# Side work of the gate and up products placed at most one split to a product, its units further apart, and w2's begun seven products into the second half

## The chip, the cores and the metric

The kernel runs on one core of one Trainium2 chip. The metric is device time in microseconds. Everything is float32; the matmuls read float32r.

## The reference

```python
x = A_x                                   # 2048 x 1024
xn = layernorm(x)
# A: linear attention, 32 heads of 32, learned feature map
q, k, v = split(xn @ wqkv)
phi(t) = concat(softmax(t @ w_phi), softmax(-(t @ w_phi)))
s = (phi(q) (phi(k)^T v) / (phi(q) sum(phi(k)) + 1e-6)) @ wo
# B: gated feed-forward, 1024 -> 3584 -> 1024
h = silu(xn @ w1) * (xn @ w3)
g = silu(h @ w2)
out = x + s * g
```

## The kernel before

**Splits.** Every float32 operand of a large matmul is used as a high and a low part: ScalarE casts the source to float32r (line 91, `hi`), VectorE subtracts that from the source (line 92, `lo`), and TensorE makes three passes over the pairs (`PASSES`). The three large products (gate and up, keys and values, the product with w2) are done in seven block products instead of eight, as Strassen and Winograd do it, so sums of blocks are needed as operands as well.

**Stages.** (1) Normalise and transpose the first half of the tokens. (2) Gate and up: `for tb in range(2)` over the two halves of the tokens, and in each `for f in range(NF)` over 28 pieces of the weights. This is where the change lies. A pass of the inner loop is called a unit here, and counted from 0 in each half. (3) Keys and values (`heads`). (4) The product with w2. (5) Queries, attention and output.

**A unit** runs the seven products of `ORDER`, named here by their activation blocks: A11, A12, S2, S1, S3, S4, A22. Each has 12 matmuls of 128x128 on 128x512. A11, S2, S3 and A22 add up in one PSUM bank (`bankb`), and it is read between them: after A11 by ScalarE (line 588), after S2 by ScalarE (line 594), after S3 by VectorE (line 603), after A22 by ScalarE (line 610). S1 and S4 share `bankc`, which ScalarE reads after S1 (line 601) and VectorE after S4 (line 605). So S3 can't start before line 594 is done, S4 not before line 601, A22 not before line 603; between a product and the one that waits for its reading lies one other product.

In each product's code come, in this order: the 12 matmuls; one split of the next unit's weights (`next(b_gen)`, tile `bo`); the side work of this product (`after`); the reading of the bank. With `in_order` every engine runs its instructions in the order of the code, so a side split that waits on ScalarE or VectorE holds back the reading of the bank behind it. Side work that TensorE does stands ahead of the matmuls (`before`).

**Side work** is what later stages need, done between these products: `side_x` (normalise, transpose and split the second half's tokens into `xo_d`), `side_fold` (fold the feature map into the query and key weights), `side_kv` (sums and splits of the key and value weights into `wkv_d`), `side_w2` (the same for w2 into `w2_d`), `side_split` (splits of `wo` and some folded weights). It is put down by a table of steps: step 7 * unit + product, from 0 to 391, the second half from `HALF` = 196. `room(step, cost)` moves a split to the next step at which `base + took + cost` is at most 2.4; `base` is 0.7 for A12, S1 and S3, 1.4 for S2 and S4, 2.1 for A22, and 2.1 or 1.4 for A11 (even and odd units). The store of a split is issued by SyncE two steps later (line 406). GpSimd does the block sums (lines 126, 127, 230 to 236, 270, 272, 457, 459, 503, 505).

**Buffers.** Every split, of the weights or of side work, writes a tile of the pool `q`, which has 11 buffers of 4 KB in each partition. A `bo` tile is held until its product in the next unit; a side tile until its store has landed. Sources of side work lie in the pool `xp` (14 buffers, first half) and in 16 places of two `room` tiles (second half). SyncE issues every DMA, in order.

Of the kernel before, what the change touches and what calls it, by code (L numbers as in the profile page):

```python
# [28 lines left out]
def tile_kernel(ctx: ExitStack, tc: tile.TileContext, x, wkT, wqT, wv, wphi, wo, w1, w3, w2, out):  # L29
# [59 lines left out]
    def split(hi, lo, src, by=None):  # L89

        nc.scalar.copy(hi, src)  # L91
        (by or nc.vector).tensor_sub(lo, src, hi.bitcast(F))  # L92
# [78 lines left out]
    def blk(name):  # L171
        return xp.tile([P, 4, P], F, name=name, tag="x")

    def flat(t):
        return t.rearrange("p k t -> p (k t)")
# [7 lines left out]
    def load_x(t, halves):  # L183
        for h in range(2):
            nc.sync.dma_start(halves[h], x[t * P:(t + 1) * P, h * 512:(h + 1) * 512])
        return halves

    def stats(mv, j, xt):
        st = small.tile([P, 2, 6], F, name="st")
        for a in range(2):  # L190
            nc.vector.bn_stats(st[:, a, :], xt[a])
        nc.vector.bn_aggr(mv[:, j], st.rearrange("p a b -> p (a b)"))

    def rstd(mv):

        sd = small.tile([P, 4, 2], F, name="sd")
        var = mv[:, :, 1]
        nc.scalar.activation(sd[:, 0], var, AF.Sqrt, bias=eps_t)
        nc.vector.reciprocal(sd[:, 1], sd[:, 0])

        nc.vector.tensor_mul(sd[:, 2], sd[:, 1], sd[:, 1])
        nc.vector.scalar_tensor_tensor(sd[:, 3], var, EPS, sd[:, 2], op0=OP.add, op1=OP.mult)
        nc.vector.tensor_scalar(sd[:, 3], sd[:, 3], -0.5, 1.5, op0=OP.mult, op1=OP.add)
        nc.vector.tensor_mul(sd[:, 1], sd[:, 1], sd[:, 3])
        return sd

    def norm(mv, sd, j, xt):

        for a in range(2):
            nc.vector.tensor_scalar(xt[a], xt[a], mv[:, j, 0:1], sd[:, 1, j:j + 1], op0=OP.subtract, op1=OP.mult)  # L210

    def turn(half):
        pt = ps.tile([P, 4, P], F, name="pt", tag="tr", bufs=3)
        for k in range(4):
            nc.tensor.transpose(pt[:, k, :], half[:, k * P:(k + 1) * P], ident)
        return pt

    def raw_x(pt):
        xf = blk("xf")
        nc.scalar.copy(xf, pt)  # L220
        return xf

    def store_x(t, hf, xf):
        nc.sync.dma_start(xn_d[:, 4 * hf:4 * hf + 4, t * P:(t + 1) * P], xf)
# [78 lines left out]
    at_fold = 0  # L303
# [59 lines left out]
    def load_kv(c, k):  # L363
        r = [flat(blk("wkv")) for _ in range(4)]
        for n in range(2):
            nc.sync.dma_start(r[n], wk_d[c][k + 4 * n])
            nc.sync.dma_start(r[2 + n], wv[(k + 4 * n) * P:(k + 4 * n + 1) * P, c * 512:(c + 1) * 512])
        return r
# [14 lines left out]
    def at(step, f, d=after):  # L383
        d.setdefault(step, []).append(f)
# [4 lines left out]
    def room(step, cost):  # L389

        while True:
            f, j = divmod(step, 7)
            base = (2.1 if f % 2 == 0 else 1.4, 0.7, 1.4, 0.7, 0.7, 1.4, 2.1)[j]
            if base + took.get(step, 0) + cost <= 2.4:
                took[step] = took.get(step, 0) + cost
                return step
            step += 1

    def store_quad(step, d, src, name):

        step = room(step, 0.7)

        def f():
            t = qp.tile(list(src().shape[:1]) + [2] + list(src().shape[1:]), R, name=name, tag="q")
            split(t[:, 0], t[:, 1], src())
            at(step + 2, lambda: nc.sync.dma_start(d, t.bitcast(F)))
        at(step, f)
        return step

    def side_x(i, s0):  # L410
        xt, a, mv, sd, pts = [], {}, [], [], {}
        t0, t1 = pairs[i]

        def load():
            xt.extend(load_x(t, [flat(blk("xt")) for _ in range(2)]) for t in (t0, t1))
            mv.append(small.tile([P, 2, 2], F, name="mv", bufs=4))

        at(s0, load)
        at_ = s0 + 2
        for j in range(2):  # L420
            at_ = room(at_ + 1, 1.6)
            at(at_, lambda j=j: stats(mv[0], j, xt[j]))
        at_ = room(at_ + 1, 1.0)
        at(at_, lambda: sd.append(rstd(mv[0])))
        for j in range(2):
            at_ = room(at_ + 1, 1.0)
            at(at_, lambda j=j: norm(mv[0], sd[0], j, xt[j]))
        s1 = at_ + 1
        for m, (n, j, hf) in enumerate((("A11", 0, 0), ("A12", 0, 1), ("A21", 1, 0), ("A22", 1, 1))):
            at(s1 + m, lambda n=n, j=j, hf=hf: pts.update({n: turn(xt[j][hf])}), before)  # L430
            at(s1 + m, lambda n=n: a.update({n: raw_x(pts[n])}))
            at(s1 + m + 2, lambda n=n, j=j, hf=hf: store_x(pairs[i][j], hf, a[n]))
        at_ = s1
        for n in ("A11", "A12"):
            at_ = store_quad(at_ + 1, xo_d[1][n][:, i - 4], lambda n=n: a[n], f"xo{n}")
        at_ = max(at_ + 1, s1 + 7)
        for m in range(3):
            at(at_ + m, lambda m=m: a_sums(a, nc.gpsimd, m))
        at_ += 1
        for n in ("S3", "S1", "S2", "S4", "A22"):  # L440
            at_ = store_quad(at_ + 1, xo_d[1][n][:, i - 4], lambda n=n: a[n], f"xo{n}")

    def side_kv(c, k, s0):
        r, t2 = [], []
        at(s0, lambda: r.extend(load_kv(c, k)))

        def sums():
            t2.append(flat(blk("t2")))
            b_sums(r[0], r[2], r[3], t2[0])

        at(s0 + 4, sums)
        at_ = s0 + 5
        for n in BNAMES:
            src = {"B11": 0, "B21": 1, "T2": 4, "T1": 0, "T3": 2, "B22": 3, "T4": 1}[n]
            at_ = store_quad(at_ + 1, wkv_d[c][n][:, :, k], lambda src=src: (r + t2)[src], "wkvo")
            if n == "B11":
                at(at_, lambda: nc.gpsimd.tensor_sub(r[0], r[3], t2[0]))
            elif n == "B21":
                at(at_, lambda: nc.gpsimd.tensor_sub(r[1], r[1], t2[0]))

    def side_fold(m, s0):
        wT, k, c, d = folds[m]
        w = []
        at(s0, lambda: w.append(load_w(wT, k, c)))
        at(s0 + 4, lambda: w.append(flat(fold(w[0], c))), before)
        if m < 16:
            at(s0 + 4, lambda: nc.scalar.copy(flat(w[0]), w[1]))
            at(s0 + 6, lambda: nc.sync.dma_start(d, flat(w[0])))
        else:
            store_quad(s0 + 4, wqo_d[c][k], lambda: w[1], "wqo")  # L470

    def side_split(d, src, s0):
        r = []

        def load():
            r.append(blk2())
            nc.sync.dma_start(r[0], src)

        at(s0, load)
        store_quad(s0 + 4, d, lambda: r[0], "wso")  # L480

    def side_w2(kb, kk, s0):
        r = []

        def load():
            r.extend(blk2() for _ in range(4))
            for h in range(2):
                f = 4 * kb + 2 * kk + h
                for n in range(2):
                    nc.sync.dma_start(r[h + 2 * n], w2[f * P:(f + 1) * P, n * 512:(n + 1) * 512])  # L490

        def sums():
            r.append(blk2())
            b_sums(r[0], r[2], r[3], r[4])

        at(s0, load)
        at(s0 + 3, sums)
        at_ = s0 + 4
        for n in BNAMES:
            src = {"B11": 0, "B21": 1, "T2": 4, "T1": 0, "T3": 2, "B22": 3, "T4": 1}[n]  # L500
            at_ = store_quad(at_ + 1, w2_d[kb][n][:, kk], lambda src=src: r[src], "w2o")
            if n == "B11":
                at(at_, lambda: nc.gpsimd.tensor_sub(r[0], r[3], r[4]))
            elif n == "B21":
                at(at_, lambda: nc.gpsimd.tensor_sub(r[1], r[1], r[4]))
# [6 lines left out]
    hs = []  # L512
    FIRST_STEP = 7
    for i in range(4, 8):
        side_x(i, FIRST_STEP + 13 * (i - 4))
    for m in range(at_fold, len(folds)):
        side_fold(m, FIRST_STEP + 6 * (m - at_fold))
    for m in range(8):
        side_kv(m // 4, m % 4, FIRST_STEP + 48 + 13 * m)
    for m in range(28):  # L520
        side_store(m, FIRST_STEP + 2 + 5 * m)

    HALF = 7 * NF
    for u in range(2 * NKB):
        side_w2(u // 2, u % 2, HALF + 1 + 11 * u)

    late_splits = [(wqo_d[c][k], d) for _, k, c, d in folds[16:at_fold]]
    late_splits += [(wo_d[c][k], wo[k * P:(k + 1) * P, c * 512:(c + 1) * 512]) for c in range(2) for k in range(ND)]
    for m, (d, src) in enumerate(late_splits):
        side_split(d, src, HALF + 11 + 11 * (m // 2) + 5 * (m % 2))  # L530

    def store_h(d, b, t):
        nc.sync.dma_start(d[:, :, b].rearrange("i p t -> p i t"), t.rearrange("p (i t) -> p i t", i=4))
# [11 lines left out]
    for tb in range(2):  # L545
        early = {}
        for f in range(NF):
            last, step = f == NF - 1, HALF * tb + 7 * f
# [352 lines left out]
    for r, new in enumerate(steps):  # L901
        kb, i = new or (NKB, 0)
# [155 lines left out]
```

## Time and profile before

| | us |
|---|---|
| median of 3 runs | 2489.83 |
| lowest and highest | 2488.6, 2492.28 |
| span of the profiled execution, first to last instruction | 2486.2 |
| gate and up, first half from unit 1's A22 on (starts at 103.23) | 529.16 |
| gate and up, second half (starts at 632.39) | 558.74 |
| keys and values begin at | 1191.13 |

The profile gives no time of that execution beyond its span. Times in the trace are microseconds from the span's start. PE is TensorE's matmul, DVE VectorE, ACT ScalarE, POOL GpSimd, SP SyncE. In a row of the timeline stand the start, the duration, the engine, the line, the operation, what is written and read, how many were merged, and in brackets the idle time before it and what ended it.

### The profile page before, as it was taken

To read this page: it belongs to the slowest core of one execution; us is meant where nothing else is said; L and a number is where in the kernel's file an instruction comes from. 1 tells how busy PE (TensorE), PEld (TensorE's weight loads), DVE (VectorE), ACT (ScalarE), POOL (GpSimd) and SP (SyncE) were. 2 spreads that over 40 slices of the span, in tenths; PEclk is the share of its full clock that TensorE was granted. 3 is DMA by queue.
4 is the path that set the end of the run, shared out by engine and by line. 5 is a ranking of instruction groups with operands and counts; after the bars stand their busy time and mean duration, and the time that the engine had idled before them with its cause. 6 is when DMAs were issued, how large, how long until landed. Compare 5 with 4: busy or idle time off the path is not lost.

```text
span 2486.2 us, 35893 instructions
## 1 busy us (share of the span) xinstructions
PE 2410.0 (97%) x13648; PEld 1969.5 (79%) x13648; DVE 1715.1 (69%) x2573; ACT 894.9 (36%) x1555; POOL 672.1 (27%) x481
## 2 busy tenths in 40 slices
PE   5999899999899999999999999999999999999999
PEld 5788678888787787788788788788888887787877
DVE  8577767664577777764466566578787876777775
ACT  6455444443344455443111113422222243222221
POOL 1244445433354554432000000011111112222222
PEclk9999999999999999999999999999999999999999
DMA  8687897755987788744966864524444276322222
GB/s 293 219 273 262 283 296 250 248 185 175 292 286 265 279 285 297 256 162 164 361 245 259 298 210 146 193 106 167 169 178 167 98 287 236 98 71 91 77 83 71
DMA packets 300812, 521.02 MB, mean 210 GB/s; under 512 B 24544, under 2 KB 172000, under 8 KB 298848
## 3 DMA queue, kind: packets, MB, share of 16 engines
q1 hardware_dynamic: 300640, 518.74, 60.2%
q8 instruction: 107, 1.75, 0.3%
q14 instruction: 65, 0.53, 0.1%
HBM read 331.22 MB, written 187.44 MB: 209 GB/s over the span
## 4 chain that ended last, share of the span: by engine, by line
PE 82%; DMA 8%; DVE 4%; issue 2%; ACT 2%; SPq 1%; POOL 1%; ACTq 0%; DVEq 0%; POOLq 0%
PE bankb L575 18%; PE pm L100 14%; PE bankb L882 12%; PE bankc L575 8%; PE bankb L659 7%; PE bankc L882 6%; PE banka L575 4%; PE bankc L659 3%; PE banka L882 3%; PE banka L659 2%; DVE bo L92 1%; DMA wkv_d0T<-wkvo 1%; PE po L986 1%; PE pkv L644 1%; PE pt L980 1%
## 5 line engine op out<-in xcount | busy, mean ns | idle before, releaser
L92 DVE TENSOR_TENSOR bo<-rw,bo 128x512 fp32r<-128x512 f32 x336 | 294.0, 876 | 142.9 <-ACT bo L91 141.7
L91 ACT CAST bo<-rw 128x512 fp32r<-128x512 f32 x336 | 205.1, 621 | 74.7 <-PE bankb L575 16.8
L882 PE MATMUL bankb<-bo,as 128*128 128x512 f32 x816 | 201.6, 390 | 3.0 <-DVE acc L894 3.0
L270 POOL TENSOR_TENSOR rw<-rw,t 128x512 f32<-128x512 f32 x56 | 78.7, 1405 | 429.8 <-DVE bo L92 429.7
L892 POOL TENSOR_TENSOR acc<-acc,u 128x512 f32<-128x512 f32 x48 | 64.0, 1334 | 479.5 <-ACT u L891 381.7
L100 PE MATMUL pm<-wq,xh 128*128 128x512 f32 x768 | 185.2, 394 | 0.0
L882 PEld LDWEIGHTS bankb<-bo,as 128*128 128x128 f32 x816 | 153.3, 188 | 35.2 <-DVE acc L894 3.4
L575 PE MATMUL bankb<-op0A,bo 128*128 128x512 f32 x672 | 161.1, 393 | 12.1 <-DVE u L603 5.7
L575 PE MATMUL bankb<-op1S,bo 128*128 128x512 f32 x672 | 164.1, 393 | 5.9 <-ACT u L594 4.8
L575 PE MATMUL bankb<-op1A,bo 128*128 128x512 f32 x672 | 159.4, 393 | 10.4 <-DVE u L603 7.6
L575 PE MATMUL bankb<-op0S,bo 128*128 128x512 f32 x672 | 163.1, 391 | 6.3 <-ACT u L594 4.8
L100 PEld LDWEIGHTS pm<-wq,xh 128*128 128x128 f32 x768 | 142.0, 188 | 31.2 <-issue 2.8
L575 PE MATMUL bankc<-op0S,bo 128*128 128x512 f32 x672 | 162.8, 391 | 2.4 <-ACT u L601 2.4
L575 PE MATMUL bankc<-op1S,bo 128*128 128x512 f32 x672 | 161.9, 390 | 1.4 <-ACT u L601 1.4
L575 PEld LDWEIGHTS bankb<-op1A,bo 128*128 128x128 f32 x672 | 126.6, 189 | 39.4 <-DVE u L603 9.8
L575 PEld LDWEIGHTS bankb<-op0A,bo 128*128 128x128 f32 x672 | 125.0, 188 | 40.4 <-DVE u L603 7.9
L575 PEld LDWEIGHTS bankb<-op1S,bo 128*128 128x128 f32 x672 | 126.4, 189 | 35.4 <-ACT u L594 7.9
L575 PEld LDWEIGHTS bankb<-op0S,bo 128*128 128x128 f32 x672 | 125.2, 188 | 33.8 <-ACT u L594 6.3
L575 PEld LDWEIGHTS bankc<-op1S,bo 128*128 128x128 f32 x672 | 126.3, 188 | 28.6 <-ACT u L601 2.3
L575 PEld LDWEIGHTS bankc<-op0S,bo 128*128 128x128 f32 x672 | 125.6, 188 | 29.0 <-ACT u L601 3.2
L882 PE MATMUL bankc<-bo,as 128*128 128x512 f32 x576 | 147.3, 391 | 0.4 <-DVE as L92 0.4
L100 PE MATMUL pm<-wos,oT 128*128 128x512 f32 x576 | 136.3, 390 | 0.0
(201 smaller groups left out, 4681.9 us busy)
## 6 DMA issues: line engine op xcount, KB each, us to landing
rw<-in_w SPq DMA_DIRECT2D x112, 512.0 KB, 5.3
h_d<-h SPq DMA_DIRECT2D x112, 256.0 KB, 7.0
hr<-h_d SPq DMA_DIRECT2D x56, 512.0 KB, 3.5
xoS<-xo_d0S SPq DMA_DIRECT2D x32, 512.0 KB, 9.5
xoS<-xo_d1S SPq DMA_DIRECT2D x32, 512.0 KB, 3.3
room<-in_w SPq DMA_DIRECT2D x56, 256.0 KB, 6.3
xoA<-xo_d0A SPq DMA_DIRECT2D x24, 512.0 KB, 9.1
xoA<-xo_d1A SPq DMA_DIRECT2D x24, 512.0 KB, 3.8
```

The source lines that it names most:

```text
L91: nc.scalar.copy(hi, src)
L92: (by or nc.vector).tensor_sub(lo, src, hi.bitcast(F))
L100: nc.tensor.matmul(p, xT[dch][:, a], w(dch, b), start=n == 0, stop=n == 3 * ND - 1)
L270: nc.gpsimd.tensor_sub(b11, b22, t2)
L575: nc.tensor.matmul(bank[b], bo[bn][:, w, k], ao[an][:, u, k], start=first and n == 0, stop=LAST[b] == an and n == 11, skip_group_check=True)
L644: nc.tensor.matmul(pkv[sl, m], e[:, m // 4, (m % 4) * P + 32 * h:(m % 4) * P + 32 * h + 32], v[:, 4 * (m % 4) + h], start=first and m == 0 ...
L659: nc.tensor.matmul(bank[b], xo[an][:, u, k], wb[bn][:, w, k], start=an in ("A11", "A12", "S1") and n == 0, stop=LAST[b] == an and n == 11, ...
L882: nc.tensor.matmul(bank[b], t[:, u, pos + k], bos[kb, bn, k][:, w], start=first and n == 0, stop=LAST[b] == an and n == 5, skip_group_chec ...
L892: nc.gpsimd.tensor_add(c, c, u)
L980: nc.tensor.transpose(pt[:, g, :], e[:, (4 * q + g) * P:(4 * q + g + 1) * P], ident)
L986: nc.tensor.matmul(po[32 * g:32 * g + 32, hh, q * P:(q + 1) * P], kvu[sl, G * c + 4 * q + g], et[sl, g], start=True, stop=True, skip_group ...
```

## The change

The side work's limits and places are other numbers; no other line differs.

```diff
     def store_quad(step, d, src, name):
-        step = room(step, 0.7)
+        step = room(step, 1.0)
...
     for i in range(4, 8):
-        side_x(i, FIRST_STEP + 13 * (i - 4))
+        side_x(i, FIRST_STEP + 16 * (i - 4))
     for m in range(at_fold, len(folds)):
-        side_fold(m, FIRST_STEP + 6 * (m - at_fold))
+        side_fold(m, FIRST_STEP + 14 * (m - at_fold))
     for m in range(8):
-        side_kv(m // 4, m % 4, FIRST_STEP + 48 + 13 * m)
+        side_kv(m // 4, m % 4, FIRST_STEP + 60 + 12 * m)
...
     for u in range(2 * NKB):
-        side_w2(u // 2, u % 2, HALF + 1 + 11 * u)
+        side_w2(u // 2, u % 2, HALF + 7 + 12 * u)
...
-        side_split(d, src, HALF + 11 + 11 * (m // 2) + 5 * (m % 2))
+        side_split(d, src, HALF + 9 + 12 * (m // 2) + 6 * (m % 2))
```

With a cost of 0.7 a step with base 0.7 took two splits, one with base 1.4 one; with 1.0 both take one. Counted over the program's order, 22 products held two side splits before, 8 in the first half and 14 in the second; now none does. The first half has 94 side splits and the second 120 in both; the last one of the first half moves from unit 22 to unit 23, those of the second half lie in units 2 to 25 instead of 1 to 22.

The first place is ScalarE in unit 6 of the second half, from the reading of A11's bank (line 588) on; `w2o` and `wso` are side splits, `bo` the next unit's weights. Before:

```order
L588 COPY h0_6383<-bankb_6365 128x512
L91 CAST bo_6398<-rw_6205 128x512
L91 CAST w2o_6402<-room_5456 128x512
L91 CAST wso_6405<-room_5456 128x512
L591 ACTIVATE h0_6383<-h0_6383 128x512
L91 CAST bo_6422<-t2_6333 128x512
L91 CAST w2o_6425<-room_5455 128x512
L594 COPY u0_6429<-bankb_6365 128x512
L91 CAST bo_6447<-rw_6205 128x512
L91 CAST w2o_6450<-room_5455 128x512
L601 COPY u1_6459<-bankc_6434 128x512
```

The same place in the changed kernel:

```order
L588 COPY h0_6355<-bankb_6337 128x512
L91 CAST bo_6370<-rw_6175 128x512
L91 CAST w2o_6374<-room_5569 128x512
L591 ACTIVATE h0_6355<-h0_6355 128x512
L91 CAST bo_6395<-t2_6305 128x512
L91 CAST w2o_6398<-room_5570 128x512
L594 COPY u0_6401<-bankb_6337 128x512
L91 CAST bo_6419<-rw_6175 128x512
L91 CAST wso_6422<-room_5569 128x512
L601 COPY u1_6427<-bankc_6406 128x512
```

A12's part, between line 588 and line 591, has one side split where it had two.

The second place is SyncE's queue where the second half begins; `op1A22` is the last activation block of that half, `room` w2's sources, `h_d` the stores that free the tiles of lines 588 and 610. Before:

```order
L162 DMA op1A22_5372<-xo_d1A22_101 128x8x128 x4
L256 DMA rw_5416<-in_w1 128x1024
L257 DMA rw_5416<-in_w3 128x1024
L490 DMA room_5455<-in_w2 128x512 x4
L533 DMA h_d0_6_64<-h0_5279 128x4x128
L533 DMA h_d0_6_64<-h1_5256 128x4x128
L533 DMA h_d0_6_64<-h1_5412 128x4x128
L256 DMA rw_5557<-in_w1 128x1024
```

and now:

```order
L162 DMA op1A22_5372<-xo_d1A22_101 128x8x128 x4
L256 DMA rw_5416<-in_w1 128x1024
L257 DMA rw_5416<-in_w3 128x1024
L533 DMA h_d0_6_64<-h0_5279 128x4x128
L533 DMA h_d0_6_64<-h1_5256 128x4x128
L533 DMA h_d0_6_64<-h1_5412 128x4x128
L256 DMA rw_5549<-in_w1 128x1024
L257 DMA rw_5549<-in_w3 128x1024
L490 DMA room_5569<-in_w2 128x512 x4
```

w2's loads stand a unit later, behind the three stores and the next weights.

The third place is SyncE's queue at the third of the key and value loads (`wkv`, in the changed kernel at step 91, unit 13 of the first half), with what each DMA waits for. Before:

```order
L366 DMA wkv_2942<-wk_d0_2_118 128x512 [waits DMAHW5_49]
L367 DMA wkv_2944<-in_wv 128x512 [waits DMAHW6_49]
L366 DMA wkv_2943<-wk_d0_6_122 128x512 [waits DMAHW7_49]
L367 DMA wkv_2945<-in_wv 128x512 [waits DMAHW0_49]
L406 DMA wkv_d0B21_103<-wkvo_2893 256x1x512 [waits DMAHW1_49,DVE_49]
L406 DMA wkv_d0T2_104<-wkvo_2918 256x1x512 [waits DMAHW2_49,DVE_49]
```

and now:

```order
L240 DMA wr_3046<-in_wqT 128x512 [waits DMAHW4_49]
L366 DMA wkv_3048<-wk_d0_2_118 128x512 [waits DMAHW5_49]
L367 DMA wkv_3050<-in_wv 128x512 [waits DMAHW6_49]
L366 DMA wkv_3049<-wk_d0_6_122 128x512 [waits DMAHW7_49]
L367 DMA wkv_3051<-in_wv 128x512 [waits DMAHW4_49,DMAHW0_49,PE_49]
L406 DMA xo_d1A22_101<-xoA22_2997 128x1024 [waits DMAHW1_49]
L406 DMA wqo_d1_3_159<-wqo_3043 128x1024 [waits DMAHW2_49,DVE_49]
L533 DMA h_d0_3_61<-h0_2890 128x4x128 [waits DMAHW3_49]
```

The load of `wkv_3051` has got the buffer of `wr_3046`, which the fold of step 95 reads, so it waits for TensorE; before, none of the four loads did.

## The prediction

> **What bounds the kernel now.** I began with the page, then went to the stretches of gate and up, the only code that the change touches.
>
> ```profile
> span 2486.2 us, 35893 instructions
> PE 2410.0 (97%) x13648; PEld 1969.5 (79%) x13648; DVE 1715.1 (69%) x2573; ACT 894.9 (36%) x1555; POOL 672.1 (27%) x481
> ```
>
> TensorE is the bound, and no matmul is taken away. What can be won is only the time in which it doesn't run. The chain of waits shows how long a unit is when nothing holds it:
>
> ```profile
> 458.47 5.44 PE bankb L575 x24
> ...
> 610.79 5.44 PE bankb L575 x24
> ```
>
> Such a row is A22 with the next A11; the two are the first and the last of nine at equal distances, so a unit is (610.79 - 458.47) / 8 = 19.04 us and a product 2.72 us. Next, the windows of the first half from unit 1's A22 on, of a stretch of it, of the second half, and of the second half's thick part (columns: length, then busy time of PE, PEld, DVE, ACT, POOL, clock, DMA share, GB/s):
>
> ```profile
> 103.23:632.39 529.16, 516.56 (x2334) 425.72 (x2333) 356.07 (x471) 240.34 (x431) 222.64 (x152) 1.00 0.76 248
> 458.47:629.83 171.36, 171.36 (x757) 141.89 (x757) 95.60 (x129) 68.50 (x124) 62.66 (x44) 1.00 0.63 202
> 632.39:1191.13 558.74, 541.03 (x2353) 442.31 (x2352) 377.08 (x463) 249.80 (x449) 242.17 (x164) 0.99 0.73 255
> 700.00:1090.00 390.00, 379.24 (x1651) 309.49 (x1650) 292.30 (x356) 193.21 (x347) 193.53 (x128) 1.00 0.78 274
> ```
>
> Second half: 28 units x 19.04 = 533.1, so **25.6 us** are lost in 558.74. First half: 183 products x 2.72 = 497.8, so 31.4 are over, part of it TensorE's own side work:
>
> ```profile
> 118.22 0.60 PE L215 MATMUL pt<-ident,xt 128*128 128x128 f32 x4
> 118.58 3.00 PE L575 MATMUL bankb<-op0S,bo 128*128 128x512 f32 x12
> ...
> 150.55 1.05 PE L247 MATMUL pw<-bd,wr 128*128 128x128 f32 x8
> 151.36 1.85 PE L575 MATMUL banka<-op0A,bo 128*128 128x512 f32 x7
> ```
>
> A group of four transposes takes 0.36 and a fold 0.81, about 0.1 more each with the restart; 16 groups and 9 folds make some 16. That leaves **15.4 us** of waits in the first half. Together 41.0 us, 1.6% of the span, is all that placing side work can win here.
>
> **Who is waited for.** TensorE's timeline in the second half: its waits over 0.5 us but one, and (677.17) unit 1's A22:
>
> ```profile
> 651.65 5.70 PE L575 MATMUL bankb<-op1A,bo 128*128 128x512 f32 x24 [2.78 <-DMA op1A<-xo_d1A]
> 669.98 4.50 PE L575 MATMUL bankb<-op1S,bo 128*128 128x512 f32 x12 [3.39 <-ACT u L594]
> 677.17 5.60 PE L575 MATMUL bankb<-op1A,bo 128*128 128x512 f32 x24
> 710.70 3.03 PE L575 MATMUL bankb<-op1S,bo 128*128 128x512 f32 x12 [0.73 <-ACT u L594]
> 777.24 7.18 PE L575 MATMUL bankb<-op1A,bo 128*128 128x512 f32 x24 [2.36 <-DVE u L603]
> 831.33 3.04 PE L575 MATMUL bankb<-op1S,bo 128*128 128x512 f32 x12 [0.67 <-ACT u L594]
> 835.36 3.03 PE L575 MATMUL bankc<-op1S,bo 128*128 128x512 f32 x12 [0.99 <-ACT u L601]
> 877.89 5.74 PE L575 MATMUL bankb<-op1A,bo 128*128 128x512 f32 x24 [0.98 <-DVE u L603]
> 936.18 5.74 PE L575 MATMUL bankb<-op1A,bo 128*128 128x512 f32 x24 [0.83 <-DVE u L603]
> 996.61 5.74 PE L575 MATMUL bankb<-op1A,bo 128*128 128x512 f32 x24 [2.53 <-DVE u L603]
> 1016.82 5.78 PE L575 MATMUL bankb<-op1A,bo 128*128 128x512 f32 x24 [0.88 <-DVE u L603]
> ```
>
> All but the first of these waits are for a bank's reading. The rows down to 677.17 lie in units 0 and 1. The others lie in units 3, 6, 9 (twice), 11, 14, 17 and 18. Against the program's order: nine units hold two side splits in A12, namely 2, 3, 6, 9, 11, 13, 14, 17 and 18. Every stalled unit after unit 1 is one of these, and seven of the nine stall; four units with their double elsewhere (4, 7, 12, 15) and all eight units from 2 to 22 without one lose next to nothing. Unit 6 shows how:
>
> ```profile
> 774.74 0.62 ACT L91 CAST w2o<-room 128x512 fp32r<-128x512 f32 x1 [1.91 <-DMA w_d1T<-w2o]
> ```
>
> S3's side split waits for a `q` buffer, that is for an earlier store to land; S3's bank is read behind it, and A22 waits. The buffers say why one split more matters: a `bo` tile lives eight products (written in one, read a unit later), so eight of the 11 are taken and three are left. Stores take
>
> ```profile
> xo_d1S<-xoS SPq DMA_DIRECT2D x16, 512.0 KB, 3.7
> xo_d1A<-xoA SPq DMA_DIRECT2D x12, 512.0 KB, 7.1
> w_d1T<-w2o SPq DMA_DIRECT2D x8, 512.0 KB, 6.7
> ```
>
> 6.7 with some 2 for the split ahead is 8.7 us or 3.2 products: three buffers carry 0.94 splits a product, 6.6 a unit, but not two in a row. In the free stretch no product has two and the densest unit has five.
>
> **The change, term by term,** against the span of 2486.2.
>
> Doubles in the second half: units 0 and 1 end one product behind 677.17, at 679.89, which is 47.5 from 632.39 where two free units take 38.1: 9.4 lost. Of the 25.6, 16.2 remain for the units behind. The order now has at most one split in a product and four to six in a full unit. Counted from the places that the two programs give to the `q` tiles, a side split whose buffer waits for a store issued in the same product occurs 14 times before and never now; at S3, waits for a store issued one product earlier fall from nine to three. I keep 4.0 for these three and four such at S1 (about 0.6 each from rows like 0.67 and 0.73). Bounds: 0, as in the free stretch, and 32, if each of 24 units lost what the dense unit of a single-split kind lost in the first half (1.35, below). I take 4.0, near the free stretch, the nearest row. **Gain 12.2.**
>
> Units 0 and 1: TensorE waited 2.78 for op1A22 and then for a backlog.
>
> ```profile
> 657.17 1.28 POOL L126 TENSOR_TENSOR room<-room 128x512 f32<-128x512 f32 x1 [18.57 <-DMA room<-in_w]
> 658.69 0.60 ACT L610 ACTIVATE h<-bankb 128x512 f32<-128x512 f32 x1 [13.08 <-DMA h_d<-h]
> ```
>
> w2's loads stood ahead of the `h_d` stores, and GpSimd's sums of w2 ahead of the weights' sums. Both now come a unit later and unit 1 holds no side split. The 2.78 stays (3.0 with the restart), since its fetch stands ahead as before; 0.4 is left for the `h_d` wait. 9.4 becomes 3.4: **gain 6.0**, with 3 and 8 as bounds.
>
> First half, what goes:
>
> ```profile
> 256.54 3.02 PE L575 MATMUL bankb<-op0A,bo 128*128 128x512 f32 x12
> ...
> 303.24 5.74 PE L575 MATMUL bankb<-op0A,bo 128*128 128x512 f32 x24 [2.04 <-DVE u L603]
> ```
>
> From unit 9's A11 to unit 10's A22 46.7 passed where 13 products and a fold take 36.3, so these two units lost 10.4 of the 15.4. They have four doubles, and casts that wait for the product running or for the one behind it:
>
> ```profile
> 271.38 0.62 ACT L91 CAST wkvo<-wkv 128x512 fp32r<-128x512 f32 x1 [2.04 <-PE bankb L575]
> 272.53 3.02 PE L575 MATMUL bankc<-op0S,bo 128*128 128x512 f32 x12 [1.19 <-ACT u L601]
> ```
>
> Three side splits had a buffer that is freed only one product later (1.35 us each with the restart); now one has, in unit 13. The bunch of GpSimd sums for tokens and keys still meets VectorE's normalising in unit 10. I leave it 2.0, between 0 and unit 10's whole 7.2, near the low end as the doubles are gone.
>
> First half, what is added: SyncE now stops at the load of `wkv_3051` from about step 91 until the fold of step 95, some four products. Behind it stand the stores of `xoA22`, `wqo` and `wkvo`, one `h_d` store and the next loads. In step 95 the weights' split needs `xoA22`'s buffer: fold 0.9, issues 1.0, landing 3.7 to 7.1, then two casts, two subtractions and line 603, 2.5 to 4.5; A22 could start at 7.7 after the step began. That is 0.4 to 5.8, I take 2.2, and 1.3 for the late buffer just before: **3.5 lost in unit 13**. GpSimd's hold (`t2` waits for a split two products on, with the weights' sums behind it) should end about a product before they are needed, at 1.3 us or more a sum (row 657.17); I take nothing, 1 at worst. In the second half the fetch of op2B21 waits two products for the last w2 split, with the last weights' load behind it. Its rows are
>
> ```profile
> 1133.92 0.43 SPq L257 DMA_DIRECT2D rw<-in_w  x1
> 1153.74 0.61 ACT L91 CAST bo<-rw 128x512 fp32r<-128x512 f32 x1
> ```
>
> with 19.8 between issue and use, so 5.4 are hidden; uncovered it would cost those 5.4.
>
> Units 14 to 23 hold five or six single splits each instead of five and one to three by turns. Unit 11, with six singles, lost 1.35 behind the bunch of units 9 and 10; units 15 to 22 lost nothing. Bounds 0 and 13; I take 2.0. The first half keeps 2.0 + 3.5 + 2.0 = 7.5 of 15.4: **gain 7.9**.
>
> Sum: 12.2 + 6.0 + 7.9 = 26.1. The span becomes 2460.1; the median lies 3.6 above the span, so **2463.7, rounded to 2464**. TensorE's work and the later stages don't move.
>
> **Rivals.** *GpSimd's bunches, not the doubles, make the stalls.*
>
> ```profile
> 287.66 1.78 DVE L92 TENSOR_TENSOR xoS<-s,xoS 128x512 fp32r<-128x512 f32 x1
> 297.48 0.68 DVE L92 TENSOR_TENSOR xoS<-xf,xoS 128x512 fp32r<-128x512 f32 x1
> ```
>
> The same subtraction takes 1.78 beside a GpSimd sum and 0.68 alone. For it: GpSimd is busy 50% in the thick part and 37% in the free stretch. Against it: w2's sums fall into every unit or second unit, and units without a double in A12 ran free. Then only units 0 and 1 are won: 2489.8 - 6.0 = 2483.8. [...]
>
> *The waits for stores are spread, not removed.* One split a product keeps the ring nearly full, and each unit loses a little; half of the second half's and first half's gain stays: 2489.8 - 6.0 - 6.1 - 4 = 2474.
>
> *Slower: dense units of single splits stall on the ring.* If unit 11's 1.35 is the rule for units of five or six, of which there are now about 31, they cost 42 where I put 6; with 3.4 + 5.5 kept, 51 against 41: +10, so 2500. It decides from about 1.0 us a unit. Against it stand units 15 to 22 and the 6.6 splits a unit worked out above.
>
> **How the numbers follow.** My forecast has 0.70 (2454 to 2473 its own range), spread waits 0.14, GpSimd's bunches 0.09, slower 0.07. The range takes in the rivals of 2474 and 2483.8 and, below, everything won but the wait for op1A22: 2452 to 2484. What a measurement here tells from no change is about 0.2%, 5 us. The forecast and the spread waits are faster, half of the third about the same: faster 0.87, same 0.06, slower 0.07.
>
> **What would show it.** Right: in the second half no TensorE wait over 1 us after unit 0, and units of 19.04 nearly throughout; no wait of line 610 on `h_d` of 13 us; in the first half one new loss, at unit 13, with SyncE stopped ahead of it. Wrong: ScalarE's casts waiting for `w_d` stores in most units with A22 late behind them (ring), or VectorE's subtractions at 1.7 ahead of each late line 603 (GpSimd).

## The result, and the profile after

| | before | after |
|---|---|---|
| median of 4 runs, us | 2491.06 | 2477.50 |
| lowest and highest | 2488.6, 2492.69 | 2475.28, 2479.13 |
| profiled execution, span | 2486.2 | 2474.2 |
| time of that execution | not on record | 2476.03 |

The ratio is 0.9945 with a 95% interval of 0.9931 to 0.9959: faster, by 13.6 us where 26.1 were forecast. The changed kernel lies inside the range (2452 to 2484), above the forecast's own 2473, and 3.5 above the rival "the waits for stores are spread, not removed" (2474).

The head of the page of after, span and busy time of each engine:

```profile
span 2474.2 us, 35921 instructions
PE 2408.9 (97%) x13648; PEld 1969.3 (80%) x13648; DVE 1718.2 (69%) x2573; ACT 896.9 (36%) x1555; POOL 668.5 (27%) x481
```

TensorE's work is the same to 1.1 us, so the 12 us are waits that went. Windows of after, in the columns of the prediction: the first half from unit 2 on, the second half, its thick part, and the second half behind unit 1.

```profile
104.85:627.02 522.17, 515.77 (x2322) 424.78 (x2320) 357.25 (x468) 241.38 (x431) 222.69 (x152) 1.00 0.76 252
627.02:1175.63 548.61, 537.97 (x2353) 441.61 (x2352) 373.14 (x463) 250.28 (x449) 241.16 (x164) 1.00 0.75 260
700.00:1090.00 390.00, 383.25 (x1681) 314.23 (x1680) 288.70 (x355) 191.03 (x343) 190.70 (x128) 1.00 0.75 263
671.15:1175.63 504.48, 497.74 (x2185) 409.05 (x2184) 353.82 (x437) 236.53 (x424) 226.36 (x153) 1.00 0.75 262
```

The second half is 548.61 long, 15.5 over its 533.1; before it was 25.6 over. Behind unit 1, 26 units take 504.48 instead of 495.04: 9.4 lost, where 16.2 were. The first half from unit 2 on is 522.17 - 495.04 = 27.1 over, and 11.2 without TensorE's side work (15.9, the prediction's "some 16"); the same sum for before gives 15.5. (The prediction's own prices, 0.46 for a group of transposes and 0.91 for a fold, make 15.6; with that every loss given for the first half would be 0.3 higher, in all kernels alike.)

TensorE's timeline of the second half of after, the rows in which it waited over 0.3 us, but one:

```profile
647.68 7.31 PE L575 MATMUL bankb<-op1A,bo 128*128 128x512 f32 x24 [3.13 <-DMA op1A<-xo_d1A]
728.37 5.76 PE L575 MATMUL bankb<-op1A,bo 128*128 128x512 f32 x24 [2.66 <-DVE u L603]
843.93 5.74 PE L575 MATMUL bankb<-op1A,bo 128*128 128x512 f32 x24 [0.44 <-DVE u L603]
959.85 5.75 PE L575 MATMUL bankb<-op1A,bo 128*128 128x512 f32 x24 [1.12 <-DVE u L603]
998.61 5.73 PE L575 MATMUL bankb<-op1A,bo 128*128 128x512 f32 x24 [0.33 <-DVE u L603]
1052.74 3.03 PE L575 MATMUL bankb<-op1S,bo 128*128 128x512 f32 x12 [2.16 <-ACT u L594]
```

They lie in units 0, 4, 10, 16, 18 and 21. No product holds two side splits now, so what is left behind unit 0 comes from single ones. Unit 4 shows how; first SyncE's queue, then the other engines (timeline):

```profile
714.56 3.10 SPq L490 DMA_DIRECT2D room<-in_w  x4
717.76 1.35 SPq L406 DMA_DIRECT2D w_d0T<-w2o  x2
```

```profile
725.79 0.62 ACT L91 CAST w2o<-room 128x512 fp32r<-128x512 f32 x1 [4.37 <-DMA w_d0T<-w2o]
725.90 1.26 POOL L127 TENSOR_TENSOR room<-room 128x512 f32<-128x512 f32 x1
726.44 1.28 DVE L92 TENSOR_TENSOR w2o<-room,w2o 128x512 fp32r<-128x512 f32 x1 [4.30 <-ACT w2o L91]
727.64 0.68 DVE L603 TENSOR_TENSOR u<-bankb,u 128x512 f32<-128x512 f32 x1
```

S3's side split waits 4.37 us for a buffer whose store stands one product earlier in the code. That store, one of the two from 717.76 on, was issued behind four loads that held the queue for 3.10, and landed 7.9 us later. The subtraction then takes 1.28 instead of 0.68 beside a sum on GpSimd, line 603 stands behind both, and A22 starts at 728.37.

How much ScalarE waited in all is in the groups of its casts behind unit 1 (after the bar: busy time, mean ns, then idle time before them). Before:

```profile
L91 ACT CAST bo<-rw 128x512 fp32r<-128x512 f32 x150 | 92.0, 620 | 26.6 <-PE bankb L575 4.8 <-DMA w_d3B<-w2o 3.6 <-DMA wo_d<-wso 2.3
L91 ACT CAST w2o<-room 128x512 fp32r<-128x512 f32 x92 | 57.1, 620 | 26.3 <-PE bankc L575 3.9 <-DMA w_d2T<-w2o 3.5 <-DMA w_d5T<-w2o 3.2
L91 ACT CAST bo<-t 128x512 fp32r<-128x512 f32 x25 | 15.2, 607 | 3.5 <-DMA w_d0T<-w2o 1.3 <-DMA w_d3T<-w2o 1.1 <-DMA w_d5B<-w2o 0.9
L91 ACT CAST wso<-room 128x512 fp32r<-128x512 f32 x22 | 13.7, 622 | 14.1 <-PE banka L575 5.5 <-issue 3.2 <-DMA w_d3B<-w2o 2.3
```

After:

```profile
L91 ACT CAST bo<-rw 128x512 fp32r<-128x512 f32 x150 | 92.8, 621 | 40.0 <-DMA w_d5T<-w2o 8.7 <-PE bankc L575 5.2 <-DMA w_d1T<-w2o 5.1
L91 ACT CAST w2o<-room 128x512 fp32r<-128x512 f32 x97 | 60.1, 620 | 19.2 <-DMA w_d0T<-w2o 4.4 <-DMA w_d5B<-w2o 3.2 <-DMA w_d4T<-w2o 2.9
L91 ACT CAST bo<-t 128x512 fp32r<-128x512 f32 x25 | 15.1, 605 | 0.0
L91 ACT CAST wso<-room 128x512 fp32r<-128x512 f32 x22 | 13.7, 621 | 11.4 <-PE bankb L575 4.1 <-DMA w_d2T<-w2o 2.4 <-DVE bo L92 1.9
```

The idle times add up to 70.5 us before and 70.6 after. Not all of that is for buffers: by what ended each wait, 48.4 us before and 51.5 after are waits for a store, most of the rest is for TensorE. So ScalarE waits for stores as long as it did; it waits in other places, more often ahead of a `bo` cast. Matching each wait with its store, over both halves: waits for a store issued in the same product fell from 11.7 us to 1.6, those for a store issued one product earlier rose from some 30 to some 55.

In the first half, unit 10 of after (timeline):

```profile
280.88 1.76 DVE L92 TENSOR_TENSOR xoS<-s,xoS 128x512 fp32r<-128x512 f32 x1
282.72 0.59 ACT L220 COPY xf<-pt 128x512 f32<-128x512 f32 x1 [2.93 <-DVE xoS L92]
283.36 1.04 PE L215 MATMUL pt<-ident,xt 128*128 128x128 f32 x4 [2.05 <-ACT xf L220]
```

Line 220 writes an `xp` buffer that the subtraction of the same product still reads; TensorE's next transposes wait for it. And unit 13 with SyncE's queue ahead of it:

```profile
333.94 0.45 SPq L366 DMA_DIRECT2D wkv<-wk_d  x1
343.38 0.33 SPq L367 DMA_DIRECT2D wkv<-in_wv  x1
343.75 0.43 SPq L406 DMA_DIRECT2D xo_d1A<-xoA  x1
344.28 0.38 SPq L406 DMA_DIRECT2D wqo_d<-wqo  x1
347.27 3.01 PE L575 MATMUL bankc<-op0S,bo 128*128 128x512 f32 x12 [1.19 <-ACT u L601]
351.09 5.78 PE L575 MATMUL bankb<-op0A,bo 128*128 128x512 f32 x24 [0.81 <-DVE u L603]
```

SyncE issues nothing from 334.4 to 343.4, 3.3 products, then the stores late; A22 follows late.

### The profile page after: what moved, and what is told of

It is laid out like the page before. It is cut to its first block, busy times and chain, and to the rows that moved or that the text cites. A ratio compares the mean times of both kernels' runs of the same rounds, so it can differ in the third digit from the quotient of the medians.

```text
span 2474.2 us, 35921 instructions
## 1 busy us (share of the span) xinstructions
PE 2408.9 (97%) x13648; PEld 1969.3 (80%) x13648; DVE 1718.2 (69%) x2573; ACT 896.9 (36%) x1555; POOL 668.5 (27%) x481
## 4 chain that ended last, share of the span: by engine, by line
PE 81%; DMA 8%; DVE 5%; issue 2%; ACT 2%; SPq 1%; POOL 1%; ACTq 0%; DVEq 0%; POOLq 0%
PE bankb L575 18%; PE pm L100 14%; PE bankb L882 12%; PE bankc L575 8%; PE bankb L659 7%; PE bankc L882 6%; PE banka L575 4%; PE bankc L659 3%; PE banka L882 3%; PE banka L659 2%; DVE bo L92 1%; PE po L986 1%; PE pkv L644 1%; DMA wkv_d1T<-wkvo 1%; PE pt L980 1%
```

## The experiments

Three theories for the missing half of the gain. **Stores**: the ring of 11 buffers is too short for splits whose stores land some 6 us after their issue (medians of after's `w_d` stores: 3.5 to 6.8), wherever they stand. **GpSimd**: the sums, beside which a subtraction of VectorE took 1.28 us instead of 0.68 (unit 4 above), set the stalls. **First half**: the new places there cost as much as they save. All timed runs were compared with before on the same chip: its medians in the four groups were 2490.14 (the rings and the kernels without sums), 2490.16 (half1_only to later_only), 2490.44 (both kv64) and 2488.88 (half0_only, half1_ring).

"Lost" below is what the traces give in the way shown above: first half from unit 2 on, units 0 and 1 of the second half, and the units behind.

| kernel | us | ratio, 95% interval | first half | units 0, 1 | behind |
|---|---|---|---|---|---|
| before | 2491.06 | | 15.5 | 9.4 | 16.2 |
| after | 2477.50 | 0.9945 (0.9931, 0.9959) | 11.2 | 6.1 | 9.4 |
| before_ring | 2480.01 | 0.9955 (0.9942, 0.9967) | 16.5 | 10.1 | 3.3 |
| after_ring | 2466.95 | 0.9906 (0.9891, 0.992) | 11.2 | 5.9 | 0.8 |
| before_nosum | 2468.46 | 0.9916 (0.9904, 0.9928) | 15.0 | 4.3 | 2.6 |
| after_nosum | 2464.83 | 0.9898 (0.9885, 0.991) | 8.9 | 7.7 | 0.0 |
| half1_only | 2477.16 | 0.9949 (0.9937, 0.9962) | 15.8 | 2.1 | 11.5 |
| half0_only | 2485.91 | 0.9986 (0.9977, 0.9995) | 8.9 | 9.2 | 14.3 |
| half1_ring | 2471.35 | 0.9926 (0.9914, 0.9938) | 18.1 | 5.3 | 1.3 |
| cost_h1 | 2486.43 | 0.9982 (0.9974, 0.9991) | 16.6 | 9.3 | 12.5 |
| starts_alone | 2489.18 | 0.9998 (0.9989, 1.0007) | 16.5 | 5.6 | 14.5 |
| later_only | 2491.45 | 1.0005 (0.9995, 1.0014) | 16.3 | 4.8 | 18.7 |
| after_kv64 | 2474.37 | 0.9929 (0.9916, 0.9943) | 8.9 | 4.8 | 14.6 |
| ring_kv64 | 2464.22 | 0.9892 (0.9879, 0.9906) | 8.2 | 5.6 | 2.1 |

**More places for the splits.** Every second of the first 100 side splits of the second half goes to two places taken from a `room` tile (its ring of sources shrinks from 16 places to 12), in both kernels:

```diff
...
+            if name in ("w2o", "wso") and puts[0] % 2 and puts[0] < 100:
+                t = more()
+            else:
                 t = qp.tile(list(src().shape[:1]) + [2] + list(src().shape[1:]), R, name=name, tag="q")
+            puts[0] += name in ("w2o", "wso")
```

> The kernel before, with two more buffers for the second half's side splits: every second one of the first 100 writes into two spare places of the room tiles instead of the pool q. Stores theory (a side split waits for a buffer, that is for an earlier store to land, and the bank's reading stands behind it): ScalarE's waits for w2's stores nearly vanish, the 16.2 us lost behind unit 1 of the second half fall below 6, and the time falls by about 10 us to 2481. Sums theory (GpSimd's sums slow VectorE's subtractions to 1.7 us, and that makes line 603 late): the 16.2 stay within 3 and the time stays at 2491.

> The changed kernel with the same two more buffers in the second half. Stores theory: the 9.4 us still lost behind unit 1 of the second half fall below 3, the time by about 6 us to 2471. Sums theory: they stay at 9 and the time at 2477.

Measured: 10.1 us off before and 10.6 off after. Windows behind unit 1, before_ring and then after_ring:

```profile
680.67:1179.05 498.38, 496.55 (x2186) 409.31 (x2184) 354.40 (x432) 229.21 (x419) 225.66 (x152) 1.00 0.73 258
```

```profile
671.82:1167.63 495.81, 495.58 (x2185) 409.68 (x2184) 356.64 (x437) 232.72 (x424) 227.92 (x153) 1.00 0.76 267
```

26 free units are 495.04. GpSimd's work is the same (225.66 and 227.92 against 224 and 226), and nearly all the stalls are gone, doubles or not. ScalarE's idle time ahead of its casts, added up as above, falls from 70.5 to 31.1 in before_ring and from 70.6 to 23.9 in after_ring. The part of it that is for stores falls from 48.4 to 26.0 and from 51.5 to 16.0. So behind unit 1 the waits for stores are needed for the stalls.

**Without w2's sums.** The four GpSimd sums of each w2 unit are left out, and w2's splits read the blocks that are there; splits, loads and stores keep their number. With its sums a w2 unit also gives up one of its five places in `room`, and its splits no longer wait for a sum.

```diff
         def sums():
-            r.append(blk2())
-            b_sums(r[0], r[2], r[3], r[4])
+            r.append(r[2])
...
-            if n == "B11":
-                at(at_, lambda: nc.gpsimd.tensor_sub(r[0], r[3], r[4]))
-            elif n == "B21":
-                at(at_, lambda: nc.gpsimd.tensor_sub(r[1], r[1], r[4]))
```

> The kernel before without w2's block sums on GpSimd: it leaves out the four sums of each of w2's 14 units and splits the plain blocks, so w2's operands are not the reference's. Sums theory: of the 16.2 us lost behind unit 1 of the second half less than 5 remain, 2479 or less. Stores theory: at least 11 remain; units 0 and 1 alone may gain some 4, so 2484 to 2488.

> The changed kernel without w2's block sums on GpSimd, which it leaves out as the run before does. Sums theory: of the 9.4 us lost behind unit 1 of the second half less than 3 remain, 2471. Stores theory: at least 7 remain, 2475 to 2478.

Measured: 21.7 us off before, 12.7 off after. Windows behind unit 1, before_nosum and then after_nosum:

```profile
672.82:1170.41 497.59, 497.00 (x2185) 409.42 (x2184) 308.99 (x432) 233.22 (x419) 143.55 (x100) 1.00 0.74 259
```

```profile
670.65:1165.69 495.04, 495.04 (x2185) 409.91 (x2184) 308.93 (x437) 236.45 (x424) 145.61 (x100) 1.00 0.76 267
```

In after_nosum TensorE doesn't stop at all in 26 units, though ScalarE still waits 44.6 us ahead of its casts; in before_nosum it waits 62.9 and TensorE loses 2.6. VectorE's group of the side splits, after and then after_nosum, shows one thing that went:

```profile
L92 DVE TENSOR_TENSOR w2o<-room,w2o 128x512 fp32r<-128x512 f32 x97 | 89.8, 926 | 14.0 <-ACT w2o L91 13.9
```

```profile
L92 DVE TENSOR_TENSOR w2o<-room,w2o 128x512 fp32r<-128x512 f32 x97 | 73.4, 757 | 4.3 <-ACT w2o L91 4.1
```

The waits for stores are the other: they fell too, from 48.4 us to 33.0 before and from 51.5 to 20.9 after. The cast that waited 4.37 in unit 4 of after waits 1.09 in after_nosum; its store was issued 1.2 us earlier in the unit and landed after 5.8 us instead of 7.9:

```profile
722.01 0.62 ACT L91 CAST w2o<-room 128x512 fp32r<-128x512 f32 x1 [1.09 <-DMA w_d0T<-w2o]
```

So this edit takes away a part of the store waits as well, and the two pairs of runs don't separate the causes cleanly. Nor does every stall need a slow subtraction. In unit 21 of after the cast is late by 3.23, the subtraction takes 0.69, and TensorE's wait of 2.16 (at 1052.74 above) is for ScalarE's reading behind the cast:

```profile
1051.58 0.62 ACT L91 CAST w2o<-room 128x512 fp32r<-128x512 f32 x1 [3.23 <-DMA w_d5B<-w2o]
1052.10 0.58 ACT L594 COPY u<-bankb 128x512 f32<-128x512 f32 x1
1052.23 0.69 DVE L92 TENSOR_TENSOR w2o<-room,w2o 128x512 fp32r<-128x512 f32 x1 [3.15 <-ACT w2o L91]
```

In units 4 and 16 the subtraction beside a sum takes 1.28 and 1.25, which adds 0.6 to waits of 2.66 and 1.12.

What is shown is that either edit nearly ends the stalls, so that the two theories, which the prediction set against each other, don't exclude one another. A cast that waits for a store lies ahead of every stall over 0.5 us behind unit 1, before and after. The sums add to it in two ways that the rows show, by a slower subtraction ahead of line 603 (1.28 us in unit 4) and by later stores (7.9 us to landing instead of 5.8); how much each of these is worth, and what the freed place and the missing wait for a sum add, wasn't separated. For the subtractions the runs give a mean of 926 ns in after and 757 in after_nosum, and single rows of 1.78 and 1.28 us beside a sum and 0.68 alone.

**The change by parts.** Only the second half's starts and limit (half1_only), only the first half's (half0_only), and the second half's with the two more places (half1_ring):

```diff
-        step = room(step, 0.7)
+        step = room(step, 1.0 if step >= HALF else 0.7)
```

with the condition turned round (`step < HALF`) in half0_only, and the starts of the other half as before.

> The second half of the change alone: one split to a product, w2's units 12 apart and begun at step 7; the first half as before. The second half gained 10.1 us in the trace of the changed kernel, the first 4.3. If the halves add up: 2480 (10 below the kernel before). If the first half's gain only showed because SyncE's queue differed, nothing changes for the second.

> The first half's part of the change alone (its starts and cost 1.0 there), the second half as before. If the first half's saving that the trace of after shows (15.5 us of waits down to 11.2) is real, this is about 4 us faster than before: 2486 us. Rival, from half1_only, which was as fast as after without it: no gain, 2489 to 2491, the first half's waits in this trace about 15 again or the gain lost behind.

> The second half's part of the change with two more places for its side splits, the first half as before. By the theory that the first half's part is worth about 4 us: 2471 against 2467 for after_ring; rival, that it is worth nothing: 2467. In the second half behind unit 1 the waits should be under 1 us, as in after_ring, by both.

half1_only was 13.0 us faster than before, as fast as after. From that alone the first half would be worth nothing. The other two say otherwise: half0_only gains 3.0, its interval ending at 0.9995, and half1_ring lies 4.4 above after_ring, at the edge of what their intervals tell apart (behind unit 1 it loses 1.3, a little over the 1 that was expected). Window of half0_only, first half from unit 2 on:

```profile
104.40:624.18 519.78, 513.88 (x2321) 423.43 (x2320) 354.33 (x468) 241.44 (x431) 221.84 (x152) 1.00 0.76 253
```

It is 2.4 shorter still than in after, and 6.7 shorter than in before. 13.0 + 3.0 = 16.0 against 13.6 (10 to 17 by the interval): the parts add up within what these runs can tell, and half1_only taken alone had misled.

Then the second half's part split again: its limit with the starts of before (cost_h1; there w2's units fall so far behind that some splits read a place of `room` that has been loaded anew, the same work on other data, and the casts behind unit 1 wait 6.4 us for GpSimd and loads, which they hardly do in the others), all new starts with the limit of before (starts_alone), and w2's units and the late splits only six steps later (later_only):

```diff
-        side_w2(u // 2, u % 2, HALF + 1 + 11 * u)
+        side_w2(u // 2, u % 2, HALF + 7 + 11 * u)
-        side_split(d, src, HALF + 11 + 11 * (m // 2) + 5 * (m % 2))
+        side_split(d, src, HALF + 17 + 11 * (m // 2) + 5 * (m % 2))
```

> The kernel before with one number changed: at most one split to a product in the second half. Doubles theory (two splits in A12 make the stalls, by the prediction): most of the gain behind unit 1 comes, 16.2 falls to about 9, 2483. Rival (the distance of the units and the later begin carry it): 16.2 stays within 3, 2488 or more.

> All the new starts of the change, but two splits to a product allowed as before. Doubles theory: the second half loses 14 or more behind unit 1, the first about as before, so 2486. Rival (distance and begin): about the time of the change, 2478.

> The kernel before with w2's units and the splits of wo begun six steps later and nothing else. If the backlog of units 0 and 1 comes from w2's loads standing ahead of the h_d stores: units 0 and 1 lose 3 to 6 instead of 9.4, 2485 to 2487. If it is the landing of op1A22 alone: they stay at 9, 2490.

3.7 us, nothing and nothing, where limit and starts together give 13.0; in the first half, too, starts_alone loses 16.5 as before does. Limit and starts need each other, by a count: a w2 unit brings 7 splits and, but for the last ones, 2 late splits come with it, so 9. With the new limit a unit of seven products has places for 5 splits (A12, S2, S1, S3, S4), and every second one for a sixth (A11): 5.5 / 7 = 0.79 a product, 8.6 in 11 products and 9.4 in 12. At 11 steps apart the splits fall behind, at 12 they fit; and at 12 with the old limit they still go in by twos. In cost_h1 no product of the second half holds two side splits, yet 12.5 us stay behind unit 1, where the doubles theory put about 9 and its rival 16. later_only wins unit 1 (units 0 and 1 lose 4.8) and loses that again behind it (18.7).

**The first half's places.** The eight units of key and value weights begin 4 steps later, which in the program's order removes the reuse of the `xp` buffer in unit 10 and SyncE's stop ahead of unit 13; with and without the two more places:

```diff
-        side_kv(m // 4, m % 4, FIRST_STEP + 60 + 12 * m)
+        side_kv(m // 4, m % 4, FIRST_STEP + 64 + 12 * m)
```

> The kernel after with two more places for the side splits of the second half (as in after_ring) and the eight wkv units of the first half begun 4 steps later (FIRST_STEP + 64 instead of + 60, still 12 apart). By the numbered order this takes away the two places in which the first half of after waits by its order: the ScalarE copy into xf that reuses an xp buffer whose VectorE split stands later (unit 10, 5.8 us with the normal turns), and SP's fold load that stands behind a load still waiting for its buffer (unit 13, 3.5). Theory: those losses belong to the places alone, so about 4 to 6 us go: 2461 to 2463 us against 2467 for after_ring, and units 10 and 13 of the first half each show under 1.5 us. Rival: the first half's side work costs what it costs wherever it stands (half1_only, without the first half's move, was as fast as after): 2466 to 2468, the same loss in other units.

> The kernel after with only the wkv units of the first half begun 4 steps later, no more places for splits. The same theory: 2477.5 less 4 to 6 = 2472 to 2474 us; rival: 2476 to 2478. With ring_kv64 it also says whether the first half's placing and the second half's places for splits add up (about 10 plus 5) or share a part.

Measured: 2.7 us off after_ring and 3.1 off after, between theory and rival; the intervals overlap in both pairs, so neither difference is clear of the noise by itself. Unit 13 loses nothing now but its fold. Unit 10 still waits (timeline of ring_kv64, in which line 613 is line 603 of the others):

```profile
286.13 5.74 PE L585 MATMUL bankb<-op0A,bo 128*128 128x512 f32 x24 [1.74 <-DVE u L613]
446.58 5.76 PE L585 MATMUL bankb<-op0A,bo 128*128 128x512 f32 x24 [1.23 <-DVE u L613]
```

Unit 10 went from 5.8 over in after to 3.9, its four groups of transposes (1.8) included, so it still loses 2.1 and the expected 1.5 was missed. Most of that fall isn't the new place: after_ring, after_nosum and half0_only, with the order of after in this half, have unit 10 at 4.2, and after's has 3.41 us at half the clock in it (last section). Another part of the wait moved on to units 15 to 18, as at 446.58. ring_kv64, at 2464.22, has the lowest time of the kernels that leave nothing out, 1.1% under before and 0.5% under after, though not clear of after_ring.

## Why the prediction was right, and where it was half wrong

The direction and the bound were right: the time fell, by waits alone, and TensorE's work stayed. The doubles were where before lost its time, but not what the loss needed, as the first row shows. Its three terms, with the losses of all traces that have the same order in that part (the losses of one kernel scatter by some 2 to 5 us from trace to trace, so one pair is too few):

| | before, forecast | before, traces | left, forecast | left, traces |
|---|---|---|---|---|
| second half behind unit 1 | 16.2 | 15.2 (2) | 4.0 | 11.8 (3) |
| units 0 and 1 | 9.4 | 9.3 (2) | 3.4 | 4.3 (3) |
| first half | 15.4 | 16.2 (7) | 7.5 | 10.0 (4) |
| sum | 41.0 | 40.7 | 14.9 | 26.1 |

The traces give a gain of 14.6, the times 13.6.

**Doubles in the second half: the step that failed.** The prediction counted seven buffer waits that would stay and took "about 0.6 each", from single rows of before, 4.0 in all, with 0 and 32 as bounds. 11.8 are left (9.4, 11.5 and 14.6 in three traces), so a gain of 3.4 where 12.2 was put, hardly more than the scatter. The step priced waits by the small ones that before showed beside its large ones. What is left in after is few and large: its units 4, 16 and 21 lose 3.0, 1.4 and 2.7. The ring argument (three buffers carry 0.94 splits a product) holds on the mean, but a store that lands 7.9 us after its issue, as in unit 4, takes longer than the 2.72 that a store issued one product earlier leaves. ScalarE's waits for stores, 48.4 and 51.5 us, say the same: spread, not removed. This is the rival that had 0.14 and named 2474.

**GpSimd's bunches** were put aside because units without a double ran free though sums fell into them. That showed only that sums alone don't stall TensorE. before_nosum took away 13.6 of the 16.2 with every double in place. The evidence was read as deciding between two causes where both can be at work.

**Units 0 and 1**: 3.4 forecast, 6.1 in after, 4.3 on the mean. The wait for op1A22 stayed, as forecast (2.78, now 3.13); unit 1 lost 0.1, as forecast, though it holds one side split (the cast at 664.71), not none. Two things that the prediction didn't have make up the size: 24 matmuls behind that wait took 7.31, not 5.7, which the last section explains, and before it lies a stop of 0.77. The sign given for it was wrong too:

```profile
652.78 0.60 ACT L610 ACTIVATE h<-bankb 128x512 f32<-128x512 f32 x1 [12.54 <-DMA h_d<-h]
```

Line 610 still waits 12.5 us for `h_d`, but unit 1 lost only 0.1, so the wait costs little there. That it would fall to nothing was wrong and wasn't needed for the term.

**First half**: gain 7.9 forecast, 6.2 in the traces, 3.0 and 4.4 by the times of half0_only and half1_ring. Unit 13's stop of SyncE, found in the order, came as described (9.0 us without an issue) and cost 2.6, its fold taken off, where 3.5 was put. Unit 10 kept 3.9 beside its transposes where 2.0 was put: in the three other traces of this order it kept 2.3 to 2.4, all with the reuse of an `xp` buffer in line 220, which wasn't seen, and the rest is the half clock of this trace. The dense units 14 to 23 lost 3.8 beside their folds (1.6 to 4.1 in the other three) where 2.0 was put, and units 11 and 12, put at nothing, 1.0 (1.8 to 2.3).

**Later stages.** The span fell by 12.0, gate and up by more, because the next stages took longer in this trace. The product with w2, before and then after:

```profile
1529.11:2089.34 560.23, 554.53 (x2510) 457.77 (x2503) 424.45 (x733) 184.85 (x328) 68.84 (x50) 1.00 0.48 175
```

```profile
1514.01:2076.99 562.98, 555.29 (x2510) 458.44 (x2503) 426.82 (x733) 185.32 (x328) 67.53 (x50) 0.99 0.49 174
```

Its code is the same, and its length lies between 560.2 and 563.4 in the 14 traces; before's is the shortest. These 2.8 us are taken as scatter of a single execution, not as a cost of the change; no run was made on it.

**Slower**: the dense units don't lose 1 us each; this rival is out. The range held because it took in the rivals, not because the sum was right; the forecast's own range, 2454 to 2473, was too narrow on the upper side. (By its own chances, faster comes to 0.885 and the same to 0.045, not 0.87 and 0.06.)

Open: why the first half's part shows 6.2 us in the traces and 3 to 4.4 in times. The profiled execution of half0_only was the fastest of its twelve (2481.21 against a median of 2485.91), which may account for it, but one trace can't show that.

## What to carry to other kernels

When a ring of buffers is short, moving its users about moves the waits; adding up the waits of the engine that needs the buffers, by what ended them (here 48.4 and 51.5 us for stores), shows it at once, and two more buffers did what a new table couldn't. Before setting two causes against each other, ask whether both are at work: taking away either can then remove the stall. And when a run leaves one cause out, measure the other one in it too; here the store waits fell with the sums. A limit on how much goes into one place and the pace at which work arrives have to be changed together: count places against demand.

## What the runs showed of the hardware

A stop of TensorE can cost more than its length. Behind the wait at 647.68 of after seven matmuls follow 0.43 us apart instead of 0.23, behind that at 777.24 of before six, and the granted clock of the traces is 0.50 there. In the rows below, TensorE's busy time stands first behind the length, the clock third from the end. After, at its wait for op1A22:

```profile
645.30:648.71 3.41, 1.03 (x5) 0.90 (x6) 1.29 (x2) 0.00 (x0) 0.00 (x0) 1.00 1.08 369
648.71:652.12 3.41, 3.41 (x10) 2.67 (x9) 0.00 (x0) 0.00 (x0) 0.87 (x1) 0.50 1.10 363
```

Before, at two waits of the prediction, 2.78 at 651.65 and 2.36 at 777.24:

```profile
647.28:650.69 3.41, 1.59 (x8) 0.97 (x6) 1.95 (x4) 0.00 (x0) 0.00 (x0) 1.00 1.15 352
650.69:654.10 3.41, 2.45 (x11) 2.06 (x12) 0.23 (x1) 0.00 (x0) 0.00 (x0) 1.00 1.04 414
773.58:776.99 3.41, 1.31 (x6) 0.75 (x4) 1.60 (x2) 1.62 (x3) 2.38 (x2) 1.00 0.98 401
776.99:780.40 3.41, 3.16 (x8) 2.48 (x9) 3.30 (x6) 0.75 (x2) 0.00 (x0) 0.50 0.45 184
```

The clock falls to 0.50 for 3.41 us in two of these, in unit 10 of the first half of after (283.49 to 286.90) and in unit 1 of the second half of before (671.17 to 674.58), and in the product with w2 of after once for 6.83 (1549.83 to 1556.66). Half of 3.41 us, 1.7, is an estimate of what such a fall costs. Measured, 24 matmuls took 7.31 (after, 647.68) and 7.18 (before, 777.24) where they took 5.70 to 5.78 behind waits without a fall: 1.4 to 1.6 more.

The length of the stop doesn't settle it. Around the 2.78 the clock stayed at 1.00, and 24 matmuls took 5.70 behind it; with the 2.36 it fell, and they took 7.18. In half0_only a longer one cost nothing more, its 12 matmuls took 3.02, as behind the 0.73 of before (3.03) (timeline):

```profile
662.70 3.02 PE L576 MATMUL bankb<-op1S,bo 128*128 128x512 f32 x12 [3.44 <-ACT u L595]
```

Before and after have 31 stops of over 0.5 us from unit 2 of gate and up to its end. None of the 21 under 2.0 us had half the clock behind it; of the 10 from 2.0 to 3.4 us four had (2.05, 2.36, 3.13 and 3.39) and six had not (2.04, 2.16, 2.53, 2.66, 2.78 and 3.03). What decides beside the length, no run tested.
